# Slot outputs as one plain matrix first, block-diagonal copy on GpSimd, row sums behind the sixth expert, fewer fillers

## The chip, the cores and the metric

The kernel runs on one core of one Trainium2 chip. A core has a matrix engine (TensorE, PE in the profile), three other engines that compute (VectorE, DVE; ScalarE, ACT; GpSimd, POOL), a sync engine (SP) that issues most transfers here, and 16 DMA engines. The metric is the device time of one execution in microseconds; the time of a kernel is the median of its runs.

## What is computed

A gated recurrence is followed by a mixture of experts with slots.

```python
f = lower_bound + (1 - lower_bound) * sigmoid(f_logit)
h = f[:, t] * h + (1 - f[:, t]) * x[:, t]        # over t; y[:, t] = h
X = y.reshape(B * S, D)                          # B, S, D = 4, 5056, 256
logits = X @ phi                                 # 32 slots: 8 experts x 4
d = softmax(logits, axis=0)                      # over all tokens
slot_input = d.T @ X                             # 32 x 256
slot_out[e] = relu(slot_input[e] @ w1[e]) @ w2[e]    # F = 1024
out = softmax(logits, axis=1) @ slot_out         # 20224 x 256
```

Every slot needs all tokens, so no output row can be written before the whole recurrence is done.

## The kernel before, in words

**Recurrence.** Tokens are taken in groups of 512 for each of the four sequences (`n_unit` = 40 units). For each unit SP loads `f_t` and `x_t`, ScalarE and GpSimd form the gate and the input, PE transposes them to channels, VectorE scans (L258), PE transposes back, forms logits, and adds to the slot sums `slot_ps`. Exponentials of all logits stay in `etall`, 128 rows (4 sequences x 32 slots) by 5056 tokens. The weights of the experts are loaded by GpSimd's queue (`load_w`, L131 for w1, L133 for w2), bit by bit during the recurrence (`W_AT`); the last six are issued at unit 36. The loads arrive in the order of issue.

**The order of work.** The kernel runs under a manual schedule: every engine executes its instructions in the order in which the program writes them, and waits on semaphores are added where tiles are shared. A matmul that is written ahead of another on PE therefore always runs ahead of it.

**The tail, on PE above all.** After the last unit the slot sums are finished (L398). `spin` (L138) issues filler matmuls that multiply a weight tile by itself into an unused half of the PSUM tile `tail`; nobody uses the values. The steps are then:

- 12 fillers of 128 columns (L515); VectorE copies `slot_ps` out (L518); four matmuls put the slot inputs on channels (L522); 12 more fillers (L531); VectorE and ScalarE scale (L533, L534). L533 reads the tile `tail`, into which the fillers write, and waits for the last of them.
- First layer: matmuls L551, relu L556 and L558. Transposes L567. The column sums L569, their reciprocal `rcs` (L577), and `rcs2` = `parity` x `rcs` (L578).
- Second layer of experts 0 to 3: L589 into `so4_ps`, copied by VectorE (L595). Experts 4 to 7, index j = 0 to 3: eight matmuls each (L599) into `so_ps`, in one accumulation. After j = 0 come the addition of `so4` (L604), the sums over slots for each token (`row_sums`, L332 and L335, 24 matmuls), 25 fillers of 32 columns (`SPINS`), and VectorE's reciprocals of the sums (L610, L611); then j = 1, 2, 3.
- `slot_bd`: the 128 rows of `so_ps` (slot outputs, once for each sequence) are scaled into a block-diagonal matrix of 128 rows by 2 x 256. Half 0 holds the rows of even sequences and zeros elsewhere (VectorE, L612), half 1 those of odd sequences (ScalarE, L613). The zeros come from `parity`, which is 1 on the rows of even sequences in column 0 and of odd ones in column 1.

**The outputs.** `pieces` and `whole` treat one sequence: `share` (L631) multiplies 32 rows of `etall` by the 32 rows of `slot_bd` that belong to the sequence. `couple` (L680) treats two sequences in one matmul with 64 rows and both halves. `rest` (L702) does the left-over tokens. VectorE and ScalarE take turns to scale the result out of PSUM by the row sums' reciprocals (L621, L625, L685, L691), and SP stores it (L657, L668, L694, L711). The order is `pieces(0, 0)` with eight stores, two `couple` of the short last block, `rest`, `whole(0, 1)`, and the remaining `couple`.

Of the kernel before, what the change touches and what calls it, by code (L numbers as in the profile page):

```python
# [9 lines left out]
F32 = mybir.dt.float32  # L10
BF16 = mybir.dt.bfloat16
AX = mybir.AxisListType
ALU = mybir.AluOpType
ACT = mybir.ActivationFunctionType
# [4 lines left out]
def kernel(  # L19
# [10 lines left out]
    nc = tc.nc  # L30
    B, S, D = x.shape
    E = moe_w1.shape[0]
    F = moe_w1.shape[2]
    NS = moe_phi.shape[1]
    SPE = NS // E
    P = 128
# [63 lines left out]
    parity = consts.tile([P, 2], F32, name="parity")  # L100
# [13 lines left out]
    store = ctx.enter_context(tc.tile_pool(name="store", bufs=1))  # L114
# [6 lines left out]
    w1_r = moe_w1.rearrange("e (p o) f -> e p o f", o=DC)  # L121
    w2_r = moe_w2.rearrange("e (p fc) d -> e p fc d", p=P)
    slot_bd = store.tile([P, 2, D], BF16, name="slot_bd")
    held = ExitStack()
    wts = held.enter_context(tc.tile_pool(name="wts", bufs=1))
    w1_sb = [wts.tile([P, DC, F], BF16, name=f"w1_sb{e}") for e in range(E)]
# [9 lines left out]
    def spin(dst, k, w):  # L136
        for _ in range(k):
            nc.tensor.matmul(dst[:, ds(0, w)], w1_sb[0][:, 0, :P], w1_sb[0][:, 0, :w],  # L138
                             start=True, stop=True, skip_group_check=True)

    SPINS = 25
    W_AT = {9: 1, 15: 1, 21: 1, 27: 1, 31: 1, 33: 1, 34: 3, 35: 1, 36: 6}
    w_next = [0]
    ctx.enter_context(tc.manual_schedule())
# [4 lines left out]
    with tc.tile_pool(name="sp2", bufs=3) as sp2, \  # L149
# [178 lines left out]
        def row_sums(i):  # L328
            t0, n_r = blocks[i]
            ew = etall[:, ds(t0, P * n_r)].rearrange("s (p r) -> s p r", r=n_r)  # L330
            for r in range(n_r):
                nc.tensor.matmul(rs_ps[:, t0 // P + r], ew[:, :, r], ones,  # L332
                                 start=True, stop=True, skip_group_check=True)
            if i == len(blocks) - 1:
                nc.tensor.matmul(rs_ps[:, n_grp * R - 1, ds(0, B // 2)],  # L335
                                 left.rearrange("s t u -> s (t u)"), pair_ones,
                                 start=True, stop=True, skip_group_check=True)
# [57 lines left out]
        def late_slots(bs):  # L395
            for r in range(R):
                for b in bs:
                    nc.tensor.matmul(slot_ps[ds(b * NS, NS), :], ets[last][:, r, b],  # L398
                                     hts[last][:, b, r],
                                     start=False, stop=r == R - 1,  # L400
                                     skip_group_check=True)
# [19 lines left out]
        for n in range(n_unit):  # L421
# [10 lines left out]
            else:  # L432
# [34 lines left out]
                if n == n_unit - 2:  # L467
                    tail = psp.tile([P, 2, G], F32, name="tail", tag="sp")
# [43 lines left out]
        slots(odd)  # L512
        late_slots([0, 1, 2])
        late_slots([3])
        spin(tail[:, 1], 12, P)  # L515
        slot_sb = hpool.tile([P, G, DC], BF16, name="slot_sb", tag="h")
        slot_sb = slot_sb.rearrange("p t o -> p (t o)").bitcast(F32)[:, ds(0, D)]
        nc.vector.tensor_copy(slot_sb, slot_ps)  # L518
# [6 lines left out]
    with tc.tile_pool(name="ew", bufs=1) as ew, \  # L525
         tc.tile_pool(name="pm", bufs=2, space=PSUM) as pm, \
         tc.tile_pool(name="pbig", bufs=1, space=PSUM) as pbig:

        rep2 = rep.rearrange("p b s -> p (b s)")

        spin(tail[:, 1], 12, P)  # L531
        sin = ew.tile([P, DC, NS], BF16, name="sin")
        nc.vector.tensor_scalar_mul(sin[:, 0], sin_ps[:, 0], omlb[:, ds(0, 1)])  # L533
        nc.scalar.activation(sin[:, 1], sin_ps[:, 1], ACT.Copy, scale=omlb[:, ds(1, 1)])  # L534

        cs1 = ew.tile([P, 1], F32, name="cs1")
        nc.vector.tensor_reduce(cs1, csum, AX.X, ALU.add)
        nc.vector.reciprocal(rrow[:, :wide_r], rs_ps[:, :wide_r])


        Q = 4
        H = F // 2
        his = []
        for q in range(E // Q):
            hi = ew.tile([P, F], BF16, name=f"hi{q}")
            for k in range(2):
                hi_ps = (psu.tile([P, H], F32, name="hi_ps", tag="up") if q == 0 else
                         pbig.tile([P, H], F32, name="hi_ps", tag=f"hi_ps{k}"))
                for o in range(DC):
                    for j in range(Q):  # L550
                        nc.tensor.matmul(hi_ps[ds(j * NS, NS)], sin[:, o],  # L551
                                         w1_sb[q * Q + j][:, o, ds(k * H, H)],
                                         start=(o == 0), stop=(o == DC - 1),
                                         skip_group_check=True)
                if k == 0:
                    nc.scalar.activation(hi[:, ds(k * H, H)], hi_ps, ACT.Relu)  # L556
                else:
                    nc.vector.tensor_scalar_max(hi[:, ds(k * H, H)], hi_ps, 0.0)  # L558
            his.append(hi)
        cs_ps = pm.tile([P, 1], F32, name="cs_ps", tag="pm")  # L560
        rcs = ew.tile([P, 1], F32, name="rcs")
        rcs2 = ew.tile([P, 2], F32, name="rcs2")
        for q in range(E // Q):
            ht_ps = psu.tile([P, FC, P], BF16, name="ht_ps", tag="up")
            hi_v = his[q].rearrange("p (c f) -> p f c", f=FC)
            for fc in range(FC):
                nc.tensor.transpose(ht_ps[:, fc], hi_v[:, fc], ident)  # L567
            if q == 0:
                nc.tensor.matmul(cs_ps, rep2, cs1, start=True, stop=True)  # L569
                src = ht_ps.rearrange("p f (j s) -> p f j s", s=NS)[:, :, :, ds(0, SPE)]  # L570
                src = bass.AP(tensor=src.tensor, offset=src.offset,
                              ap=[list(src.ap[0]), [P, FC], [NS + SPE, Q], [1, SPE]])
                dst = hid[:, :, :, ds(0, SPE)]
                dst = bass.AP(tensor=dst.tensor, offset=dst.offset,
                              ap=[list(dst.ap[0]), [Q * NS, FC], [NS + SPE, Q], [1, SPE]])
                nc.scalar.copy(dst, src)
                nc.vector.reciprocal(rcs, cs_ps)  # L577
                nc.vector.tensor_scalar_mul(rcs2, parity, rcs)  # L578
                continue
            for j in range(Q):  # L580
                s0 = (Q + j) * SPE
                src = ht_ps[:, :, ds(j * NS + s0, SPE)]
                copy = nc.scalar.copy if j % 2 == 0 else nc.vector.tensor_copy
                copy(wide[:, :, j, :, ds(s0, SPE)],
                     src.unsqueeze(2).broadcast_to([P, FC, B, SPE]))
        so4_ps = pm.tile([P, D], F32, name="so4_ps", tag="pm")
        for e in range(Q):
            for fc in range(FC):
                nc.tensor.matmul(so4_ps[ds(fc % 4 * NS, NS), :], hid[:, fc, e],  # L589
                                 w2_sb[e][:, fc],  # L590
                                 start=(e == 0 and fc < 4),
                                 stop=(e == Q - 1 and fc >= FC - 4),
                                 skip_group_check=True)
        so4 = ew.tile([P, D], F32, name="so4")
        nc.vector.tensor_copy(so4, so4_ps)  # L595
        so_ps = pm.tile([P, D], F32, name="so_ps", tag="pm")
        for j in range(Q):
            for fc in range(FC):
                nc.tensor.matmul(so_ps, wide[:, fc, j].rearrange("p b s -> p (b s)"),  # L599
                                 w2_sb[Q + j][:, fc],  # L600
                                 start=j == 0 and fc == 0, stop=j == Q - 1 and fc == FC - 1,
                                 skip_group_check=True)
            if j == 0:
                nc.tensor.matmul(so_ps, rep2, so4, start=False, stop=False,  # L604
                                 skip_group_check=True)
                for i in range(1, len(blocks)):
                    row_sums(i)
                q = n_grp * R - 1
                spin(tail[:, 1], SPINS, NS)
                nc.vector.reciprocal(rrow[:, wide_r:q], rs_ps[:, wide_r:q])  # L610
                nc.vector.reciprocal(rrow[:, q, ds(0, B // 2)], rs_ps[:, q, ds(0, B // 2)])  # L611
        nc.vector.tensor_scalar_mul(slot_bd[:, 0], so_ps, rcs2[:, ds(0, 1)])  # L612
        nc.scalar.activation(slot_bd[:, 1], so_ps, ACT.Copy, scale=rcs2[:, ds(1, 1)])  # L613


    held.close()
    with tc.tile_pool(name="pout", bufs=4, space=PSUM) as pout, \
# [9 lines left out]
        def share(op, i, b, r, k):  # L627
            t0, n_r = blocks[i]
            ew = etall[ds(b * NS, NS), ds(t0, P * n_r)].rearrange("s (p r) -> s p r", r=n_r)
            for j in range(k):  # L630
                nc.tensor.matmul(op[:, j], ew[:, :, r + j], slot_bd[ds(b * NS, NS), b % 2],  # L631
                                 start=True, stop=True, skip_group_check=True)

        def scale_of(i, b, r, k):
# [118 lines left out]
```

## Time and profile before

| | |
|---|---|
| median of 8 runs | 203.45 us (201.9 to 204.0) |
| profiled execution | 203.9 us; span from first to last instruction 202.1 us |
| TensorE clock granted, mean | 0.837 |
| PE, VectorE, ScalarE, GpSimd busy | 135.4, 146.2, 138.6, 99.2 us |
| moved by DMA | 70.74 MB, mean 350 GB/s |
| last matmul of `so_ps` ends | 148.05 us |
| first output matmul, first store issued | 149.19 us, 149.99 us |
| first `couple` matmul, its first store | 151.99 us, 155.18 us |
| last PE and last ScalarE work | 180.4 us, 182.0 us |

Times inside the profile are counted from the start of the span. A row of the stages view names a stretch and its length, then the busy time of PE, PE's weight loads, VectorE, ScalarE and GpSimd with the number of instructions, then the granted TensorE clock, the mean busy share of the DMA engines, and GB/s. A row of the chain of waits gives the start, the length, the engine, the tile written and the line. A row of a tile view gives line, engine, operation, output and inputs, the number of instructions, their shortest, median and longest duration in ns, when the first and the last start, and their shape. Engines work side by side, so a busy engine costs time only where something waits for it.

### The profile page before, as it was taken

Reading aid. Unit: us, or ns where it says so; the run is one execution under the profiler, and the core shown is the slowest. Engines: PE = TensorE matmul, PEld = TensorE weight load, DVE = VectorE, ACT = ScalarE, POOL = GpSimd, SP = SyncE. Lnnn points to the kernel's source line nnn. Section 1 sums busy time; section 2 is a strip of 40 time slices with the busy share of each in tenths; the row PEclk is TensorE's granted clock in tenths of the full one; section 3 lists DMA queues with packets and bytes.
Section 4 is the critical chain, followed back from the end, with each engine's and each line's share of the span. In section 5 each row is a group of like instructions: output and inputs, shape, how many; then the busy total and the mean of one; then the engine's idle time right before and its main releaser. Section 6 shows DMA issues by size and latency. Waiting matters only on the chain.

```text
span 202.1 us, 3018 instructions
## 1 busy us (share of the span) xinstructions
PE 135.4 (67%) x1078; PEld 97.3 (48%) x1078; DVE 146.2 (72%) x169; ACT 138.6 (69%) x195; POOL 99.2 (49%) x70
## 2 busy tenths in 40 slices
PE   0586465975769577572976776999969999960000
PEld 0365344854658466552766555675854533320000
DVE  1699897799997999997699799915248887850000
ACT  2688674999898999599987399343039889990000
POOL 2588585884979289772994759960000000000000
PEclk9999996699996999999797899999996555555555
DMA  5999999999999999999999999999519999999994
GB/s 186 415 418 422 420 422 415 418 418 316 414 419 363 370 420 416 314 416 409 413 314 388 249 187 211 212 214 214 103 45 397 427 432 418 454 422 415 457 425 211
DMA packets 17614, 70.74 MB, mean 350 GB/s; under 512 B 2096, under 2 KB 3120, under 8 KB 16704
## 3 DMA queue, kind: packets, MB, share of 16 engines
q1 hardware_dynamic: 15120, 62.13, 75.1%
q0 software_dynamic: 2336, 8.42, 21.0%
q8 instruction: 8, 0.13, 0.2%
q14 instruction: 6, 0.05, 0.1%
q10 hardware_dynamic: 144, 0.00, 0.0%
HBM read 58.23 MB, written 20.71 MB: 391 GB/s over the span
## 4 chain that ended last, share of the span: by engine, by line
PE 35%; DVE 29%; DMA 15%; issue 7%; ACT 3%; SPq 1%; ACTq 0%; DVEq 0%
DVE h L258 22%; PE op L680 12%; DMA f_t<-in_f_logit_dram 11%; PE hp L271 4%; DMA x_t<-in_x_dram 4%; DVE ht L285 4%; PE sp L225 3%; PE up L225 2%; PE op L631 2%; PE so_ps L599 2%; PE slot_ps L349 1%; PE tail L138 1%; SPq L189 1%; PE tail L332 1%; PE hi_ps L551 1%
## 5 line engine op out<-in xcount | busy, mean ns | idle before, releaser
L210 POOL TENSOR_TENSOR u_t<-s_t,x_t 128x1024 bf16<-128x1024 bf16 (+1 forms) x39 | 82.4, 2129 | 30.3 <-ACT s_t L199 21.2
L258 DVE TENSOR_TENSOR_SCAN h<-a,h,up 128x512 bf16<-128x512 f32 (+1 forms) x72 | 86.3, 1249 | 6.4 <-PE up L225 4.7
L271 PE MATMUL hp<-ident_f,h 128*128 128x128 f32 (+1 forms) x160 | 31.1, 320 | 31.2 <-DVE ht L285 18.4
L199 ACT ACTIVATE s_t<-f_t 128x2048 bf16<-128x2048 f32 (+2 forms) x23 | 38.4, 1670 | 14.4 <-DMA f_t<-in_f_logit_dram 14.3
L248 ACT ACTIVATE a<-sp,nomlb 128x1024 f32<-128x1024 bf16 (+2 forms) x46 | 43.3, 993 | 4.2 <-PE sp L225 1.6
L271 PEld LDWEIGHTS hp<-ident_f,h 128*128 128x128 f32 (+1 forms) x160 | 23.0, 208 | 41.7 <-DVE ht L285 23.0
L225 PE MATMUL sp<-ident_f,s_t 128*128 128x128 f32 x144 | 23.9, 316 | 9.4 <-ACT s_t L199 6.1
L225 PE MATMUL up<-ident_f,u_t 128*128 128x128 f32 x144 | 25.1, 302 | 0.7 <-POOL u_t L210 0.7
L225 PEld LDWEIGHTS sp<-ident_f,s_t 128*128 128x128 f32 x144 | 19.8, 164 | 10.8 <-issue 6.1
L680 PE MATMUL op<-slot_bd,etall 64*128 64x512 bf16 x62 | 24.4, 600 | 0.1
L691 ACT ACTIVATE oc<-op,rrow 128x256 f32<-128x256 f32 x60 | 22.8, 490 | 1.4 <-PE op L680 0.9
L685 DVE TENSOR_TENSOR oc<-op,rrow 128x1024 f32<-128x1024 f32 x16 | 19.3, 1222 | 4.6 <-PE op L680 4.5
L225 PEld LDWEIGHTS up<-ident_f,u_t 128*128 128x128 f32 x144 | 19.3, 158 | 1.8 <-POOL u_t L210 1.1
L285 DVE COPY ht<-hp 128x512 f32<-128x512 f32 (+1 forms) x22 | 14.7, 669 | 2.4 <-PE hp L271 2.4
L680 PEld LDWEIGHTS <-etall 64*128 64x128 bf16 x62 | 9.1, 153 | 14.1 <-issue 11.8
L285 ACT COPY ht<-hp 128x512 f32<-128x512 f32 (+1 forms) x18 | 10.4, 576 | 6.2 <-PE hp L271 6.0
L258 DVE TENSOR_TENSOR_SCAN h<-a,up 128x512 bf16<-128x512 f32 x8 | 9.3, 1207 | 0.7 <-PE up L225 0.7
L625 ACT ACTIVATE ob<-op,rrow 128x256 f32<-128x256 f32 x16 | 6.3, 480 | 1.9 <-PE op L631 1.8
L299 PE MATMUL lg<-h,phi 128*32 128x512 bf16 (+1 forms) x80 | 7.1, 400 | 0.0
L631 PE MATMUL op<-slot_bd,etall 32*128 32x256 bf16 x32 | 5.9, 340 | 1.5 <-ACT slot_bd L613 1.1
L349 PE MATMUL slot_ps<-ht,et 128*32 128x256 bf16 (+1 forms) x144 | 6.0, 289 | 0.8 <-DVE et L323 0.8
L631 PEld LDWEIGHTS <-etall 32*128 32x128 bf16 x32 | 4.3, 149 | 3.5 <-issue 1.8
(99 smaller groups left out, 116.4 us busy)
## 6 DMA issues: line engine op xcount, KB each, us to landing
f_t<-in_f_logit_dram SPq DMA_DIRECT2D x36, 512.0 KB, 10.1
x_t<-in_x_dram SPq DMA_DIRECT2D x36, 512.0 KB, 10.7
out_dram<-oc SPq DMA_DIRECT2D x6, 2048.0 KB, 12.9
w_sb<-in_moe_w_dram POOLq DMA_DIRECT2D x16, 512.0 KB, 8.0
out_dram<-oc SPq DMA_DIRECT2D x4, 896.0 KB, 5.6
out_dram<-ob SPq DMA_DIRECT2D x1, 2048.0 KB, 8.7
f_t<-in_f_logit_dram SPq DMA_DIRECT2D x4, 384.0 KB, 7.4
x_t<-in_x_dram SPq DMA_DIRECT2D x4, 384.0 KB, 6.8
```

Source lines behind the costliest of these rows:

```text
L199: nc.scalar.activation(s_t, f_t, ACT.Sigmoid, scale=-1.0)
L210: nc.gpsimd.tensor_tensor(uts[n][:, :r], s_t[:, :r], x_t[:, :r], ALU.mult)
L225: nc.tensor.transpose(ps[:, :, r], t[:, r], ident_f)
L248: nc.scalar.activation(decays[n // 2, o][:, ds(n % 2, k), :T], sp[:, ds(n % 2, k), :T, o], ACT.Identity, scale=nomlb[:, ds(o, 1)], bias=1.0)
L258: nc.vector.tensor_tensor_scan(h[:, :T, o], decays[n // 2, o][:, n % 2, :T], up[:, :T, o], hs[n - B][:, ds(used(n // B - 1) - 1, 1), o] if ...
L271: nc.tensor.transpose(hp[:n_p, r], hw[:, :n_p, r], ident_f)
L285: copy(hts[g][:n_p, b].rearrange("p r d -> p (r d)").bitcast(F32), hps.pop(n)[:n_p].rearrange("p r c -> p (r c)"))
L349: nc.tensor.matmul(slot_ps[ds(b * NS, NS), :], et[:n_p, r, b], ht[:n_p, b, r], start=(g == 0 and r == 0), stop=(g == n_grp - 1 and r == R ...
L631: nc.tensor.matmul(op[:, j], ew[:, :, r + j], slot_bd[ds(b * NS, NS), b % 2], start=True, stop=True, skip_group_check=True)
L680: nc.tensor.matmul(op[:, i_r].rearrange("p u d -> p (u d)"), ew[:, :, r + i_r], slot_bd[ds(j * 2 * NS, 2 * NS)].rearrange("s u d -> s (u d)"),
L685: nc.vector.tensor_tensor(ob[:, :, ds(r, k)].rearrange("p u r d -> p r u d"), op[:, ds(0, k)], scale[:, ds(r, k)].unsqueeze(3).broadcast_t ...
L691: nc.scalar.activation(ob[:, u, r + i_r], op[:, i_r, u], ACT.Copy, scale=scale[:, r + i_r, ds(u, 1)])
```

## The change

Four edits, all in the tail and the outputs.

- A new tile `slot_out` (128 x 256, bf16) takes the slot outputs, scaled by `rcs`, in one VectorE instruction. GpSimd then makes the two halves of `slot_bd` from it by multiplying with `parity`. `share` reads `slot_out`; `couple` and `rest` still read `slot_bd`. ScalarE's scaling and `rcs2` are gone.
- `row_sums` and the reciprocals move from behind j = 0 to behind j = 1. The addition of `so4` stays behind j = 0.
- The 25 fillers next to the row sums are gone.
- The two blocks of 12 fillers of 128 columns become two blocks of 22 fillers of 64 columns.

```diff
+    slot_out = store.tile([P, D], BF16, name="slot_out")
...
-    SPINS = 25
...
-        spin(tail[:, 1], 12, P)
+        spin(tail[:, 1], 22, P // 2)
         slot_sb = hpool.tile([P, G, DC], BF16, name="slot_sb", tag="h")
...
-        spin(tail[:, 1], 12, P)
+        spin(tail[:, 1], 22, P // 2)
         sin = ew.tile([P, DC, NS], BF16, name="sin")
...
-        rcs2 = ew.tile([P, 2], F32, name="rcs2")
...
                 nc.vector.reciprocal(rcs, cs_ps)
-                nc.vector.tensor_scalar_mul(rcs2, parity, rcs)
...
                 nc.tensor.matmul(so_ps, rep2, so4, start=False, stop=False,
                                  skip_group_check=True)
+            if j == 1:
                 for i in range(1, len(blocks)):
                     row_sums(i)
                 q = n_grp * R - 1
-                spin(tail[:, 1], SPINS, NS)
                 nc.vector.reciprocal(rrow[:, wide_r:q], rs_ps[:, wide_r:q])
                 nc.vector.reciprocal(rrow[:, q, ds(0, B // 2)], rs_ps[:, q, ds(0, B // 2)])
-        nc.vector.tensor_scalar_mul(slot_bd[:, 0], so_ps, rcs2[:, ds(0, 1)])
-        nc.scalar.activation(slot_bd[:, 1], so_ps, ACT.Copy, scale=rcs2[:, ds(1, 1)])
+        nc.vector.tensor_scalar_mul(slot_out, so_ps, rcs)
+        for u in range(2):
+            nc.gpsimd.tensor_scalar_mul(slot_bd[:, u], slot_out, parity[:, ds(u, 1)])
...
-                nc.tensor.matmul(op[:, j], ew[:, :, r + j], slot_bd[ds(b * NS, NS), b % 2],
+                nc.tensor.matmul(op[:, j], ew[:, :, r + j], slot_out[ds(b * NS, NS)],
                                  start=True, stop=True, skip_group_check=True)
```

## The prediction

> **What bounds the kernel now.** I read four views, from the end backwards: the stages (engine busy time, clock and DMA per stretch), the sync engine's stores in the timeline, the chain of waits, and the tile views of the operations that the change touches. The stages first; the last columns are granted clock, DMA share and GB/s:
>
> ```profile
> 149.00:150.00 1.00, 0.40 (x3) 0.27 (x3) 0.42 (x1) 0.49 (x2) 0.00 (x0) 1.00 0.00 0
> 150.00:151.00 1.00, 1.00 (x10) 1.00 (x10) 0.61 (x2) 0.53 (x3) 0.00 (x0) 1.00 0.16 52
> 151.00:152.00 1.00, 0.88 (x8) 0.61 (x6) 1.00 (x3) 1.00 (x4) 0.00 (x0) 1.00 0.65 230
> 152.00:154.00 2.00, 1.99 (x8) 0.95 (x8) 1.90 (x3) 2.00 (x7) 0.00 (x0) 0.82 1.05 413
> 154.00:160.00 6.00, 6.00 (x22) 2.92 (x21) 4.71 (x5) 4.85 (x14) 0.00 (x0) 0.50 1.03 420
> ...
> 190.00:200.00 10.00, 0.00 (x0) 0.00 (x0) 0.00 (x0) 0.00 (x0) 0.00 (x0) 0.50 0.98 421
> ```
>
> From 152 us to the end the DMA queues are full (share 0.98 to 1.05) while PE, VectorE and ScalarE are done by 182. Writing 20.7 MB at about 420 GB/s takes 49 us whatever the engines do. So the output phase is a block of fixed length, and the span ends when that block has been started and has run out. What can move the end is only what starts the block: the first store, issued at 149.99. The chain of waits says what that store waits for (start, length):
>
> ```profile
> 136.32 0.68 PE tail L138 x12
> ...
> 143.46 1.30 PE tail L332 x23
> 144.76 0.02 PE tail L335
> 144.78 0.64 PE tail L138 x25
> 145.42 2.64 PE so_ps L599 x24
> 148.07 0.03 issue
> 148.09 0.49 DVE slot_bd L612
> 148.62 0.04 issue
> 148.67 0.48 ACT slot_bd L613
> 149.15 0.04 issue
> 149.19 0.28 PE op L631
> ```
>
> The reader is to see three removable pieces in a chain without gaps: 25 fillers (L138 at 144.78) between the row sums and the last three experts, and two scalings of the same PSUM tile that run one after the other (L612, then L613), although the first output matmul needs only one of them. The row sums (L332) are on this chain too.
>
> **The change part by part,** against the profiled execution: 203.9 us, span 202.1, so 1.8 us lie around the span. It is 0.45 above the median of 203.45; I carry the difference over to the median.
>
> *The 25 fillers go.* They take 0.64 in the chain, and the tile view puts their starts 0.025 apart: 25 x 0.025 = 0.63. They stand on PE ahead of the rest of so_ps. Gain 0.63, if nothing else is late at that point; what would be next is the load of the last expert's w2, below.
>
> *The row sums move behind j = 1.* PE still does all of them before so_ps ends: 24 matmuls, 1.32, no gain and no cost on PE. Behind them waits VectorE's reciprocal (L610 before: 0.73 at 145.46, then 0.11), and behind that in VectorE's order the scaling of so_ps, so a late reciprocal would count. New order from 143.46: j = 1 (8 x 0.11 = 0.88) to 144.34, row sums to 145.66, j = 2 and 3 (16 x 0.11 = 1.76) to 147.42. The built program puts the signal for the reciprocals on the last row-sum matmul, so they run 145.7 to 146.6 with 0.8 us to spare: nothing. What is lost is cover: j = 1 now starts 2 us sooner, and its weights are the sixth of L133's eight loads. Those loads, from the view of that line:
>
> ```profile
> L133 POOL DMA_DIRECT2D w_sb<-in_moe_w_dram x8: 535/565/587, 118.3 to 128.6; - x8
> ...
> DMA to landing us min/median/max: 6.4/10.0/17.5
> ```
>
> The last one is issued at 128.6 and lands 17.5 later, at 146.1. One load takes 2.4 to 2.5 (0.52 MB at 212 GB/s, the page's slices from 121 to 141 us), so the sixth expert's weights, two loads earlier, lie there at about 141.2 and the seventh's at 143.7: j = 1 and j = 2 do not wait. j = 3 starts in the run before at 145.27 + 16 x 0.109 = 147.01, with 0.9 us of cover, and in the new order at 146.34: 0.2 us left. I take nothing for it; the other end is a landing some tenths later.
>
> *Fillers 12 x 128 wide become 22 x 64 wide, twice.* 128 wide they take 0.68 / 12 = 56 ns each, 32 wide 25.6 ns; a straight line gives 36 for 64 wide, and 64/128 of 56 gives 28. 22 of them: 0.62 to 0.79, against 0.68. The first block lies beside VectorE's copy of slot_ps (135.17 to 135.59), which releases the next matmul anyway: 0 to +0.1. The second is on the chain, since VectorE's L533 waits for its last filler: -0.06 to +0.11. Here a rule of the Trainium skill helps to choose: "TensorE: Matmul & The Clock Gate", "Back-to-back issue gap", gives one floor of about 25 ns for everything up to 64 columns. By that 22 fillers take 0.55, by the line through the rows 0.79. I take 28 ns, as the 32-wide row sits on that floor. Together -0.05; range -0.15 to +0.2.
>
> *The hand-over to the outputs.* Before: VectorE 0.48, signal, ScalarE 0.47, signal, PE at 149.19, that is 1.12 after so_ps ended. After: one scaling on VectorE of the same form (128x256 to bf16 from PSUM), signal, PE: 0.02 + 0.48 + 0.05 = 0.55. The `rcs2` step (0.23 at 140.61) was beside ScalarE's copies: nothing. Gain 0.57. What else VectorE and ScalarE wait for before their first eviction is weight loads that landed at 146.1.
>
> *The block-diagonal copy on GpSimd.* Two 128x256 multiplications, bf16 from bf16. No such row exists; the nearest ones, from the tile views of phi, left and wide:
>
> ```profile
> L111 POOL TENSOR_SCALAR phi<-phi_f,omlb x2: 354/806/1258, 6.4 to 7.6; 128x32 bf16<-128x32 f32 x2
> L342 POOL COPY left<-etall x4: 249/254/321, 133.5 to 134.5; 32x64 bf16<-32x64 bf16 x4
> L503 POOL MEMSET wide<- x1: 3582/3582/3582, 130.0 to 130.0; 128x4096 bf16 x1
> ```
>
> Memset: 0.87 ns an element; L210's two-input multiplication: 2129 / 1024 = 2.1. So one takes 0.35 + 224 x 0.87 = 0.55 to 0.35 + 224 x 2.1 = 0.82; the pair 1.1 to 1.6, or 2.5 if the first is as slow as phi's first (1.26). I take 1.4, ready 1.5 after slot_out. Its reader is the first couple's matmul (L680), at 151.99 before: 2.8 after the first output matmul and so 2.85 after slot_out. Hidden, with 0.35 to 1.7 to spare; without that cover each us late would delay the couples. The skill speaks against this step: "GPSIMD Engine Reference", "Engine selection", sends elementwise multiplications to VectorE. By that rule two scalings would stand on VectorE ahead of the first eviction; at 0.23 to 0.41 each (its copies L584 with 128 and L595 with 256 elements) they would cost 0.5 to 0.8 on the chain; by the rows GpSimd, which has nothing after L342 at 134.7, costs 0. I go by the rows. GpSimd's own queue holds nothing behind it, and the first store's wait on GpSimd is, in the built program, for older work.
>
> Sum: -0.63 - 0.57 - 0.05 = -1.25. Span 200.85, time 202.65 in the profiled execution's terms, 202.2 on the median.
>
> **The rivals.** *The last weights hold j = 3.* For: only 0.2 us of cover remains and loads and engines are not locked to each other. Against: the landing of this run fits. Landing 0.3 to 0.6 later takes that less 0.2: 202.4 to 202.6; with all of the fillers' 0.63 swallowed, 202.85. Chance 0.14.
>
> *The granted clock falls sooner.* It drops to 0.5 at about 153.3, with PE busy all through; in the 3.4 us ahead PE ran only matmuls of 32 and 64 rows. The skill's clock page ("HAM oscillation") ties a drop to idle gaps of over 3.4 us; here the longest gap of the stage is 1.1, so by the page nothing happens, and by the row work on few rows is enough. After the change full-row work ends 0.7 sooner and few-row work starts 1.2 sooner, so the drop could come one step of 3.4 us earlier, at 149.9, in the midst of the first pieces. Then some 8 piece matmuls take 0.21 instead of 0.11, partly behind the evictions, and five matmuls of the first couple 0.43 instead of 0.22: up to 1.5 later. DMA has slack there: the pieces' 2.1 MB last until about 156.4, and the couples' first store at 155.18 would move data from 155.8, so 0.6 is free. Cost 0.9, time 203.1. Chance 0.13.
>
> *Slower: the GpSimd copy is late.* Place: the first couple. Its price is us for us once the pair ends over 2.85 + 0.6 after slot_out. It has to eat 1.25 first, and to be slower by over 0.5% another 1.0: a pair of 5.7, 2.8 each. At 3 each, 6.1 with the signal: +1.4, 204.85. No GpSimd row of that size exists (2.13 for four times the elements), so 0.08 with all else that could make it slower.
>
> *The change does more:* later clock drop relative to the pieces, fillers at 25 ns: 201.7. Chance 0.07.
>
> **How the numbers follow.** The likeliest case, 0.58, gives 202.2, most of it between 201.8 and 202.6. The executions of one kernel spread over 201.9 to 204.0, which the median holds to some tenths. Range 201.5 to 203.3: it takes in the weight and clock cases and leaves out the slow GpSimd. 0.5% (about what a measurement of this kernel can tell from no change) is 1.02, so faster needs 202.43 or less: from the likeliest 0.49, from the better case 0.07, from the weight case 0.02: 0.58. Slower 0.08, the rest 0.34.
>
> **What would show it.** The chain after should read row sums, 16 so_ps matmuls, one VectorE scaling, op, with op starting near 147.95 and the first store near 148.75; no wait ahead of the last 8 so_ps matmuls; GpSimd's pair over before 149.6; DMA full from about 150.8. Wrong would be: op at 147.95 but a dip in DMA share around 154 (GpSimd or clock), L533 later than 137.1 (fillers), or a gap in so_ps at 146.3 (weights).

## The result, and the profile after

The changed kernel takes 201.1 us (median of 11 runs, 200.6 to 202.27); the kernel before, run beside it, 203.29 (32 runs). The ratio is 0.9938, with a 95% interval from 0.9912 to 0.9964; it is taken over undisturbed runs alone and so is not the quotient of the two medians (it puts the kernel before at about 202.4). 0.62% of 203.3 is 1.26 us; the interval is 0.7 to 1.8 us. A second measurement (after_again below) gave 0.996 (0.9929 to 0.999), that is 0.8 us, 0.2 to 1.4. The profiled execution took 201.45 us, its span 199.7.

The chain of waits of the changed kernel, from the second filler block to the first output matmul (start, length, engine, tile, line; line numbers differ from those before by one or two):

```profile
134.66 0.66 PE tail L139 x22
...
141.75 0.87 PE so_ps L597 x8
142.62 1.30 PE tail L332 x23
143.93 0.03 PE tail L335
143.96 1.78 PE so_ps L597 x16
145.74 0.03 issue
145.76 0.49 DVE slot_out L610
146.26 0.04 issue
146.30 0.28 PE op L630
```

The 25 fillers are gone, the row sums stand behind j = 1, and one scaling leads to the first output matmul: 0.56 after the end of so_ps, not 1.12. What this part is worth is best read as the interval from the end of the last slot-sum matmul (L398) to the first output matmul, since everything in it is fixed by the program: 135.10 to 149.19 before, 133.44 to 146.30 after, so 14.10 against 12.86. The span fell by more, 2.4, because the recurrence ahead of it ended 1.66 sooner in this execution. Nothing in that part was changed; in the 14 profiles of this study it ends anywhere from 133.1 to 135.1. That is why spans of single profiles are not compared below.

The stages (last columns: granted clock, DMA share, GB/s):

```profile
146.00:147.00 1.00, 0.37 (x2) 0.25 (x2) 0.65 (x2) 0.24 (x1) 0.58 (x1) 1.00 0.00 0
...
148.00:149.00 1.00, 1.00 (x7) 0.58 (x5) 1.00 (x3) 1.00 (x4) 0.26 (x1) 0.68 0.73 255
149.00:150.00 1.00, 1.00 (x4) 0.36 (x4) 0.64 (x2) 1.00 (x4) 0.00 (x0) 0.50 0.91 351
...
152.00:154.00 2.00, 1.81 (x7) 0.60 (x6) 2.00 (x2) 1.63 (x5) 0.00 (x0) 0.50 0.85 328
154.00:160.00 6.00, 6.00 (x24) 3.21 (x22) 4.92 (x6) 5.08 (x14) 0.00 (x0) 0.50 1.02 428
```

Two things differ from before. The clock falls to half at 148.4, only 2.1 us after the first output matmul (before: 4.1). And DMA has a hole between 152 and 154: share 0.85, where the kernel before has 1.07 in the stage that lies as far behind its first output matmul (154.9 to 156.9). The first couple's store is issued 6.91 us after the first output matmul instead of 5.99, and the pieces' data has run out by then. From the first output matmul to the last DMA packet it takes 51.6 us, before 51.2. So from the last slot-sum matmul to the last packet the two profiles differ by 0.8, not by 1.24.

GpSimd's copy, from the tile view of slot_bd (shortest, median, longest ns; first and last start):

```profile
L612 POOL TENSOR_SCALAR slot_bd<-slot_out,parity x2: 916/921/926, 146.4 to 147.3; 128x256 bf16<-128x256 bf16 x2
```

It ends at 148.26; the first couple matmul starts at 149.11 and waits for nothing but its place on PE. The last weights are in time too:

```profile
L134 POOL DMA_DIRECT2D w_sb<-in_moe_w_dram x8: 535/562/585, 116.5 to 127.0; - x8
...
DMA to landing us min/median/max: 7.0/10.4/17.3
```

127.0 + 17.3 = 144.3, and j = 3 starts at 144.69.

### The profile page after: what moved, and what is told of

Same layout as the page of the kernel before. It is cut to its first block, busy times and chain, and to the rows that moved or that the text cites. A ratio compares the mean times of both kernels' runs of the same rounds, so it can differ in the third digit from the quotient of the medians.

```text
span 199.7 us, 3008 instructions
## 1 busy us (share of the span) xinstructions
PE 133.6 (67%) x1073; PEld 96.0 (48%) x1073; DVE 146.1 (73%) x168; ACT 138.2 (69%) x194; POOL 100.8 (50%) x72
## 4 chain that ended last, share of the span: by engine, by line
PE 36%; DVE 27%; DMA 15%; issue 7%; ACT 3%; SPq 1%; ACTq 0%; DVEq 0%
DVE h L258 21%; PE op L679 12%; DMA f_t<-in_f_logit_dram 11%; PE hp L271 5%; DVE ht L285 5%; DMA x_t<-in_x_dram 4%; PE sp L225 4%; PE op L630 3%; PE so_ps L597 2%; PE up L225 2%; ACT oc L690 1%; PE tail L332 1%; PE slot_ps L349 1%; SPq L189 1%; PE hi_ps L551 1%
## 5 line engine op out<-in xcount | busy, mean ns | idle before, releaser
L679 PE MATMUL op<-slot_bd,etall 64*128 64x512 bf16 x62 | 25.0, 621 | 0.2 <-ACT oc L690 0.2
L225 PE MATMUL up<-ident_f,u_t 128*128 128x128 f32 x144 | 24.0, 292 | 0.7 <-POOL u_t L210 0.7
L225 PEld LDWEIGHTS up<-ident_f,u_t 128*128 128x128 f32 x144 | 18.6, 153 | 2.0 <-POOL u_t L210 1.1
L612 POOL TENSOR_SCALAR slot_bd<-slot_out,parity 128x256 bf16<-128x256 bf16 x2 | 1.8, 921 | 13.4 <-DVE slot_out L610 13.4
L630 PE MATMUL op<-slot_out,etall 32*128 32x256 bf16 x32 | 6.1, 353 | 1.0 <-DVE slot_out L610 0.6
```

What stands on the lines that cost most here:

```text
L225: nc.tensor.transpose(ps[:, :, r], t[:, r], ident_f)
L630: nc.tensor.matmul(op[:, j], ew[:, :, r + j], slot_out[ds(b * NS, NS)], start=True, stop=True, skip_group_check=True)
L679: nc.tensor.matmul(op[:, i_r].rearrange("p u d -> p (u d)"), ew[:, :, r + i_r], slot_bd[ds(j * 2 * NS, 2 * NS)].rearrange("s u d -> s (u d)"),
```

## The experiments

The theory was that the gain is two pieces off the chain, fillers 0.64 and hand-over 0.56, and that width, row sums and copy are worth nothing. The table has, from the traces: the interval just described (us); then, all counted from the first output matmul, when the clock fell, when the first couple's store was issued, when PE's last 16 KB instruction load started (explained with d), and when DMA ended. The ratio is to the kernel before, which ran beside each; single profiles scatter in the last four time columns, as the clock falls at another place in each.

| run | interval | clock falls | couple's store | load | DMA end | ratio (95%) |
|---|---|---|---|---|---|---|
| before | 14.10 | 4.1 | 5.99 | -1.7 | 51.2 | |
| changed | 12.86 | 2.1 | 6.91 | -0.7 | 51.6 | 0.9938 (0.9912 to 0.9964) |
| after_again | 12.88 | 1.9 | 6.98 | -1.1 | 51.7 | 0.9960 (0.9929 to 0.9990) |
| a_spins25 | 13.50 | 2.3 | 6.91 | -2.0 | 51.6 | 0.9981 (0.9952 to 1.0010) |
| b_old_handover | 13.45 | 1.1 | 7.69 | -2.2 | 52.4 | 0.9969 (0.9944 to 0.9995) |
| c_sums_j0 | 12.87 | 4.9 | 5.98 | -1.1 | 51.2 | 0.9900 (0.9843 to 0.9957) |
| d_fill12 | 12.92 | 2.7 | 6.90 | +3.1 | 52.5 | 0.9980 (0.9955 to 1.0005) |
| d_fill12_again | 12.92 | 1.9 | 6.97 | +3.0 | 52.8 | 0.9999 (0.9975 to 1.0023) |
| k_fill12_pad | 12.91 | 2.1 | 6.97 | -0.1 | 51.7 | 0.9941 (0.9917 to 0.9966) |
| e_gap_fill | 12.90 | 2.7 | 6.93 | -0.9 | 51.6 | 0.9934 (0.9909 to 0.9959) |
| f_no_fill2 | 12.27 | 2.6 | 6.90 | +3.5 | 52.5 | 0.9967 (0.9946 to 0.9988) |
| j_move_fill2 | 12.27 | 2.7 | 6.94 | +0.4 | 51.6 | 0.9936 (0.9910 to 0.9961) |
| g_copy_x3 | 12.88 | 4.9 | 9.66 | -0.8 | 54.3 | 1.0092 (1.0050 to 1.0134) |
| h_copy_vector | 12.88 | 4.6 | 6.36 | -0.7 | 51.6 | 0.9956 (0.9924 to 0.9989) |

**a: the 25 fillers back.**

```diff
                 q = n_grp * R - 1
+                spin(tail[:, 1], 25, NS)
```

> The changed kernel with the 25 fillers of 32 columns put back behind the row sums (now behind j = 1). Theory (the gain is the sum of two pieces taken off PE's chain, 0.64 for the fillers and 0.56 for the hand-over): from the last slot-sum matmul to the first output matmul 12.86 + 0.64 = 13.50 us, where the changed kernel has 12.86 and the kernel before 14.09; time 0.6 above the changed kernel, ratio to the kernel before about 0.997. Rival (the fillers' place is covered by the load of the last w2, so taking them out gave nothing): interval 12.9 and ratio 0.994, as in the changed kernel.

The interval is 13.50, 0.64 more, to the hundredth what the theory had; the ratio is 0.998. In the chain the fillers stand where they stood before, ahead of the remaining experts:

```profile
143.72 1.30 PE tail L332 x23
145.03 0.03 PE tail L335
145.05 0.64 PE tail L139 x25
145.69 1.77 PE so_ps L597 x16
```

The weights were no cover: the rival falls by the interval. The ratio alone would not settle it, as its interval and the changed kernel's overlap.

**b: the old hand-over.**

```diff
...
+                nc.vector.tensor_scalar_mul(rcs2, parity, rcs)
...
-        nc.vector.tensor_scalar_mul(slot_out, so_ps, rcs)
-        for u in range(2):
-            nc.gpsimd.tensor_scalar_mul(slot_bd[:, u], slot_out, parity[:, ds(u, 1)])
+        nc.vector.tensor_scalar_mul(slot_bd[:, 0], so_ps, rcs2[:, ds(0, 1)])
+        nc.scalar.activation(slot_bd[:, 1], so_ps, ACT.Copy, scale=rcs2[:, ds(1, 1)])
...
```

`share` reads `slot_bd` again.

> The changed kernel with the old hand-over alone: slot_bd's two halves scaled by VectorE and then ScalarE, every output matmul reads slot_bd, no GpSimd copy. Theory: last so_ps matmul to first output matmul 1.12 instead of 0.56, so the interval from the last slot-sum matmul is 13.42; ratio to the kernel before about 0.9966. Rival (the first pieces don't set the end, the first couple does, and it waits for something else): interval 13.4 but the time of the changed kernel, ratio 0.994. Rival clock (the GpSimd version loses part of its gain as TensorE is slower in the first couples): also near 0.994 to 0.995, with less of a dip in DMA share after the pieces than the changed kernel's profile had (0.85 in the two us ahead of the couples' first store).

```profile
145.03 1.78 PE so_ps L599 x16
...
146.84 0.49 DVE slot_bd L612
...
147.42 0.48 ACT slot_bd L613
...
147.94 0.28 PE op L631
```

Interval 13.45, 0.59 more; ratio 0.997, again with an interval that overlaps the changed kernel's. The two scalings are in series again. This profile also shows what an early fall of the clock costs: at 1.1 after the first output matmul the couple's store is at 7.69 and DMA ends 1.2 later than with a fall at 4.1. So the clock's hole does not belong to GpSimd's version.

**c: row sums behind j = 0.** The condition `j == 1` becomes `j == 0`.

> The changed kernel with row sums and reciprocals back behind j = 0 (the fillers stay out). Theory: the move is worth nothing, as all row sums are on PE ahead of the end of so_ps either way and the reciprocals are hidden either way; interval 12.86, ratio 0.994. Rival (the move is what pays, because weights come late or the reciprocals hold VectorE): interval longer by 0.2 or more, with a gap in so_ps matmuls or a later scaling.

Interval 12.87: the move is worth nothing on the chain, as the sum had it. The ratio is lower, on six runs, and its interval overlaps the changed kernel's. Its clock fell late, at 4.9, and the stage that has the hole in the changed kernel has none here, with DMA's end back at 51.2:

```profile
152.00:154.00 2.00, 2.00 (x6) 0.74 (x6) 1.43 (x3) 1.64 (x5) 0.00 (x0) 0.50 1.07 424
```

**d: both filler blocks 12 x 128 again.** The edit stands in both places.

```diff
-        spin(tail[:, 1], 22, P // 2)
+        spin(tail[:, 1], 12, P)
```

> The changed kernel with both filler blocks as before, 12 of 128 columns. Theory: the two blocks together 0.03 to 0.1 longer (each 0.68 to 0.78 instead of 0.66 to 0.75), interval 12.9, ratio 0.994. Rival (narrow fillers let the granted clock fall in the tail in some executions): a profile like the changed kernel's and a time below it by 0.3 or more.

> The changed kernel with the two filler blocks of 12 x 128 once more, now on one chip with the changed kernel. Theory (the width is worth 0.06): interval 12.92, time within 0.1 of the changed kernel. Rival (the width carries most of the gain, as the first measurement of 0.998 would have it): 0.8 above the changed kernel, with a step of the tail that is longer in the trace.

The interval is right, 12.92. The time is not: 0.998, and 1.000 beside the changed kernel's 0.996 on one chip (after_again, expected at 0.994). The chain shows no longer step; the drain does. Stages of the second run, and its first eight stores in the tile view of ob:

```profile
149.00:150.00 1.00, 1.00 (x4) 0.36 (x4) 0.59 (x1) 1.00 (x4) 0.00 (x0) 0.50 1.08 392
150.00:151.00 1.00, 1.00 (x4) 0.43 (x4) 0.79 (x1) 0.32 (x1) 0.00 (x0) 0.50 0.33 121
151.00:152.00 1.00, 1.00 (x6) 0.41 (x3) 0.52 (x2) 0.93 (x3) 0.00 (x0) 0.50 0.34 132
```

```profile
L656 SPq DMA_DIRECT2D out_dram<-ob x8: 332/430/2209, 147.1 to 152.2; - x8
```

DMA runs nearly dry from 150 to 152, since one store's issue took SP 2.2 us (149.02 to 151.23), where the longest in the changed kernel took 0.79. At 149.21, inside that time, the trace has a packet of 16 KB that took 1.64 us on the queue that the page calls "instruction". There are eight of these in every run, and the eighth is ahead of the first store in the changed kernel (at -0.7) and among the stores here (+3.0). Ahead of the first output matmul the traces have 1983 weight loads and matmuls on PE in the changed kernel, 1993 before, and 1943 here: a filler is one of each, and d has 20 fillers less. (The expectations below count the program's own instructions, 1493 and 1453: the same difference.) In all 14 profiles the eighth packet starts when PE has started 1967 to 2011 of them, whether the first output matmul comes sooner or later. New theory: the packets are PE's instruction loads, fewer instructions ahead of the outputs push the eighth into the drain, and a store whose issue meets it hangs.

**k: the same 12 x 128, with 20 fillers of 32 columns in the gap where PE waits for slot_out.**

```diff
+        spin(tail[:, 1], 20, NS)
         nc.vector.tensor_scalar_mul(slot_out, so_ps, rcs)
```

> The kernel with both blocks of 12 x 128 again (which measured 0.998 and 1.000), with 20 fillers of 32 columns added behind the last so_ps matmul, where PE waits 0.56 us for slot_out; so PE has as many instructions ahead of the first output matmul as in the changed kernel (1493; without the 20 it has 1453). Theory (PE's eighth 16 KB instruction load lies among the first stores when PE has 40 instructions less ahead of them, and a store's issue then hangs for 1.5 to 2.2 us): the load comes back to about 0.7 us ahead of the first output matmul, no store issue is over 0.8, and the time is that of the changed kernel, ratio 0.994 to 0.996. Rival (the width of the fillers itself carries the difference, by the clock or else): ratio 0.998 to 1.000 as before; 20 x 25 ns fit the gap, so nothing is added.

```profile
150.00:151.00 1.00, 1.00 (x3) 0.31 (x3) 0.56 (x1) 0.60 (x2) 0.00 (x0) 0.50 1.07 420
151.00:152.00 1.00, 1.00 (x5) 0.43 (x3) 0.66 (x1) 0.71 (x2) 0.00 (x0) 0.50 1.01 409
...
L657 SPq DMA_DIRECT2D out_dram<-ob x8: 332/432/874, 147.4 to 151.0; - x8
```

The load is back at -0.1, no issue is over 0.87, DMA ends at 51.7, the ratio is 0.994 instead of 0.998 and 1.000; its interval lies below that of the second d and overlaps that of the first by a little. Twenty useless matmuls in a gap are worth about 0.9 to 1.1 us of DMA's end here. The rival, that the width itself matters, falls. That the hanging issue is due to the load rests on their coming together in the three profiles with a late load (longest of the first eight issues 2.21, 1.54 and 1.99, and at most 0.88 in the eleven others) and on this run; how the one holds up the other no trace shows.

**f: the second filler block left out. j: moved into the gap, as 22 of 32 columns.** f deletes the `spin` ahead of `sin`; j does that and puts `spin(tail[:, 1], 22, NS)` ahead of the scaling of so_ps.

> The changed kernel without the second block of fillers (between the matmuls that put the slot inputs on channels and their scaling). Theory (L533 waits for the last filler, so the block is on the chain): interval 12.86 - 0.66 = 12.20, ratio 0.9905. Rival (the fillers hold the clock up for the first layer): the interval grows or stays, as the first-layer matmuls run at half clock, 2.1 us becoming up to 4.2.

> The changed kernel with the second filler block moved: out of the chain ahead of L533, and in its place 22 fillers of 32 columns behind the last so_ps matmul, in the gap in which PE waits for slot_out. PE's instruction count ahead of the outputs stays 1493. Theory (0.66 of the chain goes, and the instruction load stays ahead of the stores): interval 12.86 - 0.6 = 12.25 and a drain as in the changed kernel; 0.6 below the changed kernel, ratio 0.990 to 0.992. Rival (taking that block out costs something of its own, as in the run that left it out and gained only 0.1 at a 0.6 shorter interval): ratio 0.995 to 0.997.

Both have the interval of 12.27, 0.59 less: L533 does wait for the last filler, and the clock stays at 1.00 without the block. In f the load slips to +3.5, a store's issue takes 1.99, and DMA ends 0.9 later, so the gain is lost again (0.9967). In j the load is at +0.4, ahead of the first data, and DMA ends as in the changed kernel. By the trace j is 0.6 shorter than the changed kernel; its ratio of 0.9936 doesn't tell it from the changed kernel's 0.9938 and 0.996, nor from k's 0.9941 on the same chip. Both ratios lie above what was expected (0.9905 for f, 0.990 to 0.992 for j). In f the late load goes with it; for j no trace shows a cause, and its interval still takes in part of what was expected. Whether j beats the changed kernel stays open.

**e: fillers in the gap, to hold the clock.** `spin(tail[:, 1], 5, D)` ahead of the scaling of so_ps.

> The changed kernel with 5 fillers of 256 columns on all 128 rows put behind the last so_ps matmul, into the 0.56 us in which PE waits for slot_out. Clock theory (the clock falls one step of 3.4 us after a stretch in which PE streamed under about 3000 full-array columns): the fall comes at the earliest 2.6 us after the first output matmul instead of 1.9, the hole in DMA is smaller or gone; time 0 to 0.3 below the changed kernel. Rival (the fall is set by the drain's matmuls alone, or costs nothing): same time; if the fillers hold back the first output matmul, up to 0.1 more.

The clock falls at 2.7, as this theory had it, but the hole is the same (share 0.85 from 153 to 155), with DMA's end at 51.6; the first output matmul is not held back. The ratio of 0.9934 is below after_again's 0.996 on that chip, but the intervals overlap: inconclusive.

**g: GpSimd's copy three times over.** `for u in (0, 1) * 3`.

> The changed kernel with GpSimd's pair of copies done three times over (same values), 5.5 us instead of 1.84. Theory (the pair is hidden up to about 2.85 us after slot_out, and DMA has data of the pieces for some 7 us after the first output matmul): the first couple starts 5.7 us after the first output matmul instead of 2.8, its store at about 9 to 9.8, DMA has a hole of about 3 us; 2.3 to 2.9 above the changed kernel, ratio 1.006 to 1.009. Rival (the drain has room to take up a late start of the couples): under 1 us, ratio under 0.999.

```profile
152.00:153.00 1.00, 1.00 (x4) 0.44 (x4) 0.35 (x1) 0.00 (x0) 0.00 (x0) 0.50 1.05 407
153.00:154.00 1.00, 1.00 (x5) 0.37 (x3) 0.88 (x1) 0.50 (x2) 0.00 (x0) 0.50 0.28 105
154.00:155.00 1.00, 0.94 (x4) 0.21 (x2) 0.64 (x1) 1.00 (x4) 0.00 (x0) 0.50 0.00 0
155.00:156.00 1.00, 0.88 (x3) 0.42 (x4) 1.00 (x2) 0.81 (x3) 0.00 (x0) 0.50 0.00 0
```

The first couple starts at 5.61 instead of 2.81, and DMA stands empty from about 153.3 to 156.5; it ends 2.7 later than in the changed kernel, ratio 1.009. The cover is real and has an edge: the couple is 2.8 late, and 2.7 of it are paid.

**h: the copy on VectorE.** `nc.gpsimd` becomes `nc.vector` in that line.

> The changed kernel with the block-diagonal copy on VectorE instead of GpSimd, written at the same place, so ahead of the first eviction. Theory: two instructions of 0.2 to 0.4 us stand between slot_out and VectorE's first eviction; first store 0.4 to 0.8 later, ratio 0.996 to 0.998. Rival (VectorE is quicker than that on bf16 and ScalarE's half of the pieces hides it): within 0.2 of the changed kernel.

```profile
L612 DVE TENSOR_SCALAR slot_bd<-slot_out,parity x2: 279/282/285, 146.3 to 146.5; 128x256 bf16<-128x256 bf16 x2
```

VectorE does the pair in 0.48 where GpSimd takes 1.84, but ahead of its first eviction: first store 1.23 after the first output matmul instead of 0.86. Against c, whose clock also fell late, DMA ends 0.43 later. Ratio 0.9956, in its interval not apart from the changed kernel's.

## Why the prediction was right, point by point

- **Sum.** Forecast -1.25; the trace's interval has -1.24, and that is where the forecast was made and holds. That the ratio gives -1.26 is luck to the hundredth: its interval is 0.7 to 1.8 us, the second measurement gave 0.8, and the two profiles, with the drain taken in, differ by 0.8. The median of 201.1 lies below 201.5, the low end of the range. The forecast took its gain off 203.45, the median of eight runs, where the ratio puts the kernel before at about 202.4; 0.9938 of 203.45 is 202.2. So the gain was forecast well and the level about 1 too high.
- **25 fillers:** -0.63 forecast, 0.64 by a. **Hand-over:** -0.57 forecast, 0.59 by b. **Row sums:** nothing forecast, 0.01 by c. These are differences of single profiles; in the times, where the intervals overlap, the parts can't be told apart.
- **Filler width:** on the chain -0.05 forecast, 0.06 by d. The 22 fillers took 0.66, 30 ns each: between the 0.55 of the 25 ns floor and the 0.79 of the line through the rows, and a little over the 28 ns taken. But "together -0.05" was the wrong account of this edit. It kept 40 instructions on PE ahead of the outputs, and without them 0.9 to 1.2 us go to a hole in DMA (d against the changed kernel: 52.5 and 52.8 against 51.6). The prediction has no term for this. The total held because the changed kernel is only 10 instructions shorter there than the one before, which is luck. For the same change with the old widths, which is d, the same sum would have given -1.2, where 0.998 and 1.000 were measured.
- **GpSimd copy:** 1.4 taken for the pair, 1.84 measured, outside the 0.55 to 0.82 for one but still hidden, with 0.85 to spare. The Trainium skill's "GPSIMD Engine Reference", "Engine selection", sends such a multiplication to VectorE. VectorE was quicker (0.28 against 0.92 for one), but the place there would have cost about 0.4 by the profiles of h and c; the times don't tell h from the changed kernel. The rows were the better guide to the place, though not to the duration.
- **Last weights:** 0.2 of cover forecast, 0.4 in the profile. No wait. The forecast's own new order gives 0.4 too: j = 2 from 145.66 and 0.88 put j = 3 at 146.54, not 146.34. And a landing 0.3 late, less 0.2, makes 202.3, not 202.4.
- **Clock:** the rival came true in the profiled execution: a fall at 2.1, the couple's store 0.9 later where up to 1.5 was forecast, a hole, and 0.4 lost where 0.9 was. As far as these profiles show it is no cost of the change: the fall comes in steps of 3.4 us that lie differently in each execution (1.1 to 4.9), and it came soonest in b, which has the old hand-over. With one profile of the kernel before, how often each falls early was not measured.

## What to carry to other kernels

When a kernel ends in a block of transfers of fixed length, cost a change by what starts the block, and then look whether the block stays full: a hole is paid nearly in full (2.7 us in g, about 1 us in d). Count instructions, not only their time: fillers that look worthless can decide where an engine's instruction load falls, and a load among the stores cost more here (0.9 to 1.2) than the 25 fillers did (0.64). A useless instruction in a gap cost nothing in k and e (intervals 12.91 and 12.90); the same instruction on the chain does.

## What the runs showed of the hardware

- A 16 KB instruction load that fell among the stores came with one store issue of 1.5 to 2.2 us instead of 0.3 to 0.9 (d, f), and DMA ended 0.9 to 1.2 us later. In all 14 profiles that load started at nearly the same place in PE's order of instructions.
- The granted clock falls to half, and stays there for the whole drain (PE busy 1.00 from 154 to 170 in the changed kernel), though no gap between matmuls from 14 us ahead of the outputs to the fall was longer than 0.57 in the changed kernel and 1.14 before. The Trainium skill's "TensorE: Matmul & The Clock Gate" ("HAM oscillation") speaks of idle gaps of over 3.4 us; none that long stands in this stretch.
- One count sorts the steps around the outputs (those that ended from 3.4 us ahead of the first output matmul up to the fall). Count the columns of the matmuls that start in a step of 3.4 us, each weighted by the share of the 128 rows in use. Over the 14 profiles, steps with 448 to 2816 (2176 in the changed kernel, 2432 before, 2624 in b) were followed by half clock, and steps with 3136 (c) and more, 3456 before, were not. By this count the earliest fall is at about 0.9 us after the first output matmul with the old hand-over and at about 1.6 with the new, where so_ps ends closer to it: an estimate from the traces of before, b, c and the changed kernel. But the count does not sort the steps of the recurrence: in the changed kernel one with 4096, which ended at 49.4, was followed by half clock, and one with 1664, which ended at 63.0, was not. So it is no rule, and what sets the clock stays open.
- GpSimd took 0.92 us for one multiplication of 256 bf16 elements a partition (changed kernel), VectorE 0.28 (h).
